# Attention before a routed expert layer: rounds of two score chunks, transposes a stage ahead, masks and shifts moved to other engines, one transfer for v

## The chip, the cores and the metric

One core of one Trainium2 chip. The metric is the device time of one execution in microseconds (us), the median of several; a profile of one execution goes with each kernel. Ratios between kernels are the mean time of one kernel's runs over that of the other's runs of the same rounds, so a ratio is not quite the ratio of the medians quoted beside it. Executions over 1.5% slower than the fastest of the same kernel are left out of the means.

Engines in the profile: PE is TensorE's matmuls, PEld its weight loads, DVE VectorE, ACT ScalarE, POOL GpSimd, SP SyncE; a q after a name means the engine's sequencer, which issues DMAs. In these traces an engine works through its own instructions in a fixed order: the two traced executions of the kernel before, almost 8 us apart in span, have the same order on every engine.

## The reference, cut to what matters

```python
B, H, S, D = 4, 8, 768, 64            # batch, heads, sequence, head width
scores = q @ k.T / sqrt(D)
# heads 0, 2, 6 ("retrieval"): causal mask
# heads 1, 3, 4, 5, 7 ("streaming"): causal, and only the last 64 keys or the first 4 ("sinks")
a = softmax(where(mask, scores, -1e9));  attn = a @ v
x = attn as [3072 tokens, 512]
out[tokens of expert e] = relu(x @ w1[e]) @ w2[e]     # 8 experts, 512 -> 1024 -> 512, one per token
```

## The kernel before

Heads go in pairs. For each pair q and k are transposed by TensorE and copied to SBUF, the on-chip memory for tiles (q by ACT, k by DVE; the copies are called qT and kT). Scores come out transposed (keys on the partitions), ACT takes the exponential, DVE multiplies by a mask, TensorE multiplies by v, which carries a column of ones for the sum of the row (this product is called AV below). The routing decides the slot of every token; POOL scatters the normalized rows there, the experts load them back slot by slot. "Pairs" are (0,2), (6,7), (1,3), (4,5), in that order, one stage each:

```python
def load_v(b):                                   # twelve transfers, issued by POOL
    for par in range(2):
        for t in range(NSO):
            nc.gpsimd.dma_start(out=ves[b][:, t, 4 * par : 4 * par + 4, 0:D], in_=v[b, par::2, ...])

def s_retr_pair(b, pi, c):                       # one chunk of scores of a causal pair
    ...                                          # 64-row matmuls of both heads into sc
    nc.scalar.activation(out=et[:, :, 448 * c : 448 * c + 448], in_=sc[:, :, 0:448], func=AF.Exp, scale=scale)
    for J in range(NSO):                         # the diagonal blocks' mask
        if 448 * c <= OFF[J] < 448 * c + 448:
            d = et[:, :, OFF[J] : OFF[J] + P]
            nc.vector.tensor_tensor(out=d, in0=d, in1=m_diag..., op=ALU.mult)

def vshift(b):                                   # v moved by 64 keys, for the streaming heads
    nc.vector.tensor_copy(out=vshs[b][0:64, ...], in_=ves[b][0:64, ...])
    nc.vector.tensor_copy(out=vshs[b][64:128, ...], in_=ves[b][64:128, ...])       # two of these

for b in range(B):
    ...
    for si, chunks in enumerate(stages):
        tq = t_units(b, si + 1) if si < 3 else (t_units(b + 1, 0) if b + 1 < B else [])
        per = -(-len(tq) // len(chunks)) if tq else 0
        for ci, (bud, f) in enumerate(chunks):
            f()                                  # scores, exponential, mask of one chunk
            for _ in range(per): ...             # transposes of the NEXT stage's pair
            run_a(bud)                           # some AV matmuls of earlier stages
        ...
        if si == 0: vshift(b)
...
load_w(wA, 2)                                    # POOL: weights of expert 2
load_x(0); load_x(1)                             # SP: rows of the first two experts
x_transpose(0)
load_w(wB, 3)
```

The softmax here doesn't subtract the row's maximum and nothing guards it: scores larger than these inputs give would overflow.

## Time and profile before

| | before |
|---|---|
| median of 4 runs | 269.31 us (268.14 to 271.21) |
| the profiled execution | 276.72 us, span 275.1 us |

From the profile's page of the kernel before: the span; busy time and share of each engine; TensorE's busy tenths in 40 equal slices; and the clock that TensorE was granted, in tenths of full speed.

```profile
span 275.1 us, 4932 instructions
...
PE 196.7 (72%) x1979; PEld 109.9 (40%) x1979; DVE 120.9 (44%) x340; ACT 92.5 (34%) x109; POOL 120.8 (44%) x191
...
PE   0279178783578478757600399999999999999940
...
PEclk9999999655696558855955569999999999999995
```

A slice is 6.9 us. The left half (to about 138 us) is attention, the two empty slices are the passage to the experts, and the rest is the experts at 90% and more. In attention no engine is full, and the clock is at 5 or 6 tenths most of the time. (The first digits of the clock row say nothing: this trace has no clock record before 46.6 us, and the transposes there took 0.31 us each, as in later stretches at half clock, against 0.22 at full clock.)

The waits of TensorE in attention, from the list of who waited for whom (total us, times, longest):

```profile
PE scs_2_0_453 L301 <- DVE kT_2_439 L218: 6.2, 1, 6.2
...
PE scs_2_0_946 L301 <- DVE kT_2_932 L218: 5.3, 1, 5.3
...
PE scs_2_0_1490 L301 <- DVE kT_2_1461 L218: 3.1, 1, 3.1
...
PE scs_2_0_1951 L301 <- DVE kT_2_1926 L218: 2.4, 1, 2.4
```

All four are the scores of the third stage, one per batch, waiting for DVE's copy of the transposed k. The timeline around the first (start, length, engine, line, what; idle time and its cause in brackets):

```profile
26.42 0.53 PE L205 MATMUL tpk_2_404<-ct,k_132 128*64 128x128 f16 x6
...
31.25 0.17 DVE L557 CAST r_loh<-r_lo 128x24 f16<-128x24 f32 x1
31.33 0.89 DVE L289 TENSOR_TENSOR eT_0_354<-eT_0_354,ct 128x128 f16<-128x128 f16 x6
32.14 0.55 DVE L340 TENSOR_TENSOR eS_0_416<-eS_0_416,m_str 128x768 f16<-128x768 f16 x1
32.61 0.95 DVE L218 COPY kT_2_439<-tpk_2_404 128x768 f16<-128x768 f16 x1
...
33.62 0.54 PE L301 MATMUL scs_2_0_453<-qT_2_388,kT_2_439 64*64 64x128 f16 x12 [6.22 <-DVE kT_2_439 L218]
```

The transposes were done at 27, the copy came at 32.6: it stood in DVE's queue behind a part of the routing (small operations until 31.4, the cast is the last of them) and then two sorts of masks. TensorE reached the scores and found no kT. In batch 1 the queue was held up otherwise, by a mask that waited for ACT's exponential:

```profile
64.76 0.56 DVE L340 TENSOR_TENSOR eS_1_909<-eS_1_909,m_str 128x768 f16<-128x768 f16 x1 [3.81 <-ACT eS_1_909 L337]
65.24 0.95 DVE L218 COPY kT_2_932<-tpk_2_895 128x768 f16<-128x768 f16 x1
```

### The profile page before, as it was taken

Reading aid. Unit: us, or ns where it says so; the run is one execution under the profiler, and the core shown is the slowest. Engines: PE = TensorE matmul, PEld = TensorE weight load, DVE = VectorE, ACT = ScalarE, POOL = GpSimd, SP = SyncE. Lnnn points to the kernel's source line nnn. Section 1 sums busy time; section 2 is a strip of 40 time slices with the busy share of each in tenths; the row PEclk is TensorE's granted clock in tenths of the full one; section 3 lists DMA queues with packets and bytes.
Section 4 is the critical chain, followed back from the end, with each engine's and each line's share of the span. In section 5 each row is a group of like instructions: output and inputs, shape, how many; then the busy total and the mean of one; then the engine's idle time right before and its main releaser. Section 6 shows DMA issues by size and latency. Waiting matters only on the chain. (4 is left out here: it accounts for less than half of the span.)

```text
span 275.1 us, 4932 instructions
## 1 busy us (share of the span) xinstructions
PE 196.7 (72%) x1979; PEld 109.9 (40%) x1979; DVE 120.9 (44%) x340; ACT 92.5 (34%) x109; POOL 120.8 (44%) x191
## 2 busy tenths in 40 slices
PE   0279178783578478757600399999999999999940
PEld 0235045352344255444500245544554545454410
DVE  0835953874799654976720103141413141413120
ACT  1186067333585158625000032404150505051400
POOL 8579398584725840242464001535344440504140
PEclk9999999655696558855955569999999999999995
DMA  7999999957999549510119999899999998202030
GB/s 134 236 172 137 182 60 170 155 98 141 193 203 138 97 85 187 95 60 19 50 70 168 239 230 224 206 213 270 213 276 229 272 229 215 112 4 92 17 112 1
DMA packets 55731, 41.27 MB, mean 150 GB/s; under 512 B 27901, under 2 KB 49301, under 8 KB 55703
## 3 DMA queue, kind: packets, MB, share of 16 engines
q0 software_dynamic: 50096, 35.67, 78.9%
q1 hardware_dynamic: 5606, 5.24, 6.9%
q8 instruction: 16, 0.26, 0.4%
q14 instruction: 13, 0.10, 0.1%
HBM read 56.64 MB, written 11.53 MB: 248 GB/s over the span
## 5 line engine op out<-in xcount | busy, mean ns | idle before, releaser
L400 POOL DMA_INDIRECT x_slots<-xb_1111,dest_i x6 | 6.7, 1122 | 23.1 <-DVE xb_1111 L451 20.9
L177 POOL DMA_DIRECT2D ve_1097<-in_v_dram x12 | 9.0, 772 | 10.0 <-DMA w_0_943<-in_moe_w_dram 3.7
L715 PE MATMUL tpx_0_2304<-ct,xe_2297 128*128 128x128 f16 x8 | 1.0, 311 | 16.8 <-DMA xe_2297<-x_slots 16.8
L177 POOL DMA_DIRECT2D ve_159<-in_v_dram x12 | 9.3, 804 | 4.8 <-DMA k_156<-in_k_dram 3.1
L177 POOL DMA_DIRECT2D ve_141<-in_v_dram x12 | 9.0, 762 | 4.9 <-DMA q_131<-in_q_dram 2.6
L749 POOL DMA_INDIRECT out_dram<-ob_2404,idx_i x1 | 1.0, 1049 | 22.8 <-DVE ob_2404 L748 22.8
L742 ACT ACTIVATE hT_2329<-h_0_0_2330 128x896 f16<-128x896 f32 x1 | 0.9, 917 | 30.0 <-PE h_0_0_2330 L735 30.0
L177 POOL DMA_DIRECT2D ve_600<-in_v_dram x12 | 8.9, 772 | 4.4 <-DMA k_597<-in_k_dram 3.1
L400 POOL DMA_INDIRECT x_slots<-xb_1633,dest_i x6 | 5.8, 972 | 6.4 <-DVE rcps_1_2183 L443 3.4
L715 PEld LDWEIGHTS <-xe_2297 128*128 128x128 f16 (+1 forms) x16 | 1.4, 138 | 17.1 <-DMA xe_2297<-x_slots 16.9
L400 POOL DMA_INDIRECT x_slots<-xb_614,dest_i x6 | 6.5, 1083 | 3.0 <-DVE xb_614 L451 1.8
L400 POOL DMA_INDIRECT x_slots<-xb_245,dest_i x6 | 6.1, 1024 | 1.5 <-issue 1.1
L719 DVE COPY xT_2303<-tpx_0_2304 128x1024 f16<-128x1024 f16 x1 | 0.7, 691 | 13.4 <-PE tpx_0_2304 L715 13.4
L488 PE MATMUL dom_ps<-ct,r_dlow 24*128 24x24 f16 x1 | 0.2, 197 | 8.3 <-DVE r_dlow L484 8.3
L735 PEld LDWEIGHTS <-w_0_941 128*128 128x128 f16 x32 | 3.8, 119 | 5.4 <-issue 3.8
L301 PE MATMUL scs_2_0_453<-qT_2_388,kT_2_439 64*64 64x128 f16 (+2 forms) x12 | 0.5, 311 | 6.2 <-DVE kT_2_439 L218 6.2
L719 DVE COPY xT_2370<-tpx_0_2371 128x1024 f16<-128x1024 f16 x1 | 0.7, 692 | 9.3 <-PE tpx_0_2371 L715 9.3
L749 POOL DMA_INDIRECT out_dram<-ob_3152,idx_i x1 | 1.0, 971 | 7.8 <-DVE ob_3152 L748 7.8
L749 POOL DMA_INDIRECT out_dram<-ob_3021,idx_i x1 | 1.0, 971 | 7.7 <-DVE ob_3021 L748 7.7
L735 PEld LDWEIGHTS <-w_1_1485 128*128 128x128 f16 x32 | 3.1, 98 | 3.0
L735 PEld LDWEIGHTS <-w_5_2578 128*128 128x128 f16 x32 | 3.1, 98 | 3.0
L735 PEld LDWEIGHTS <-w_7_2831 128*128 128x128 f16 x32 | 3.1, 98 | 3.0
(875 smaller groups left out, 650.8 us busy)
## 6 DMA issues: line engine op xcount, KB each, us to landing
x_slots<-zt SPq DMA_DIRECT2D x8, 128.0 KB, 8.0
w_0_941<-in_moe_w_dram POOLq DMA_DIRECT2D x1, 1024.0 KB
w_0_943<-in_moe_w_dram POOLq DMA_DIRECT2D x1, 1024.0 KB
w_1_1485<-in_moe_w_dram POOLq DMA_DIRECT2D x1, 1024.0 KB
w_1_1487<-in_moe_w_dram POOLq DMA_DIRECT2D x1, 1024.0 KB
w_2_2271<-in_moe_w_dram POOLq DMA_DIRECT2D x1, 1024.0 KB
w_2_2273<-in_moe_w_dram POOLq DMA_DIRECT2D x1, 1024.0 KB
w_3_2325<-in_moe_w_dram POOLq DMA_DIRECT2D x1, 1024.0 KB
```

What stands on the lines that cost most here:

```text
L177: nc.gpsimd.dma_start(out=ves[b][:, t, 4 * par : 4 * par + 4, 0:D], in_=v[b, par::2, t * P : (t + 1) * P, :].rearrange("h p d -> p h d"),)
L301: yield lambda g=g, a0=a0, a1=a1, hp=hp: nc.tensor.matmul(out=dst[hp : hp + 64, a0 - c0 : a1 - c0], lhsT=kT[b, pi][rows, 64 * g : 64 * g + ...
L400: ins = nc.gpsimd.indirect_dma_start(out=xs_dram, out_offset=bass.IndirectOffsetOnAxis(ap=dest_i[:, t : t + 1], axis=0), in_=xbs[b][:, it, :],
L488: nc.tensor.transpose(out=dps[:], in_=dlow[:], identity=ident[0:NT, 0:NT])
L715: nc.tensor.transpose(out=ps[:, j, c, 0:n], in_=xe[e][0:n, g, c * P : (c + 1) * P], identity=ident[0:n, 0:n])
L719: nc.vector.tensor_copy(out=xT[e][:, :, 0:256].rearrange("p c (j n) -> p c j n", j=2), in_=ps[:].rearrange("p j c n -> p c j n"),)
L735: nc.tensor.matmul(out=sc[:, j, 0:CAP], lhsT=w1t[:, c, ft * P : (ft + 1) * P], rhs=xT[e][:, c, :], start=(c == 0), stop=(c == 3),)
L742: nc.scalar.activation(out=hT[e][:, 2 * fp : 2 * fp + 2, :], in_=sc[:, :, 0:CAP], func=AF.Relu)
L749: ins = nc.gpsimd.indirect_dma_start(out=out, out_offset=bass.IndirectOffsetOnAxis(ap=idx_i[:, col : col + 1], axis=0), in_=ob[:], in_offs ...
```

## The change: intent and diff

The scores go in rounds: two chunks' score matmuls, then the masks of both, then both exponentials, then other work of TensorE ("fills"), so that matmuls of one tile shape stand side by side. The pairs' order is now (1,3), (4,5), (6,7), (0,2), and a pair's transposes are made a stage or more ahead, most of them in the last rounds of the batch before. The causal mask becomes a matmul that adds -30000 (identity times a mask block) to the scores in PSUM, the memory that TensorE writes its results to; the v shift goes from DVE to POOL, one scaling per streaming block from DVE to ACT. v of a batch comes by one transfer. Warm-up matmuls of zeros stand at the start and before the experts. The routing's arithmetic gets shorter. The diff, cut to its core (cuts are `...`):

```diff
-PAIRS = [(0, 2), (6, 7), (1, 3), (4, 5)]
+PAIRS = [(1, 3), (4, 5), (6, 7), (0, 2)]
...
-    c16[:, 128:256] = pp[:, None] <= pp[None, :]
+    c16[:, 128:256] = np.where(pp[:, None] <= pp[None, :], 0.0, NEG)
...
     def load_v(b):
-        for par in range(2):
-            for t in range(NSO):
-                nc.gpsimd.dma_start(... one sixth of four heads ...)
+        nc.gpsimd.dma_start(
+            out=ves[b][:, :, :, 0:D].rearrange("p h t d -> p (h t) d"),
+            in_=v[b].rearrange("h (t p) d -> p (h t) d", p=P),
+        )
...
+        def mask(n):
+            a0 = diag[n] - p0
+            nc.tensor.matmul(
+                out=dst[:, a0 : a0 + P], lhsT=ident, rhs=m_diag, start=False, stop=(n == len(diag) - 1)
+            )
...
-            for J in range(NSO):
-                if 448 * c <= OFF[J] < 448 * c + 448:
-                    d = et[:, :, OFF[J] : OFF[J] + P]
-                    nc.vector.tensor_tensor(... op=ALU.mult)
...
+    def run_round(chunks, fills):
+        for prods, _, _, _ in chunks:
+            prods()
+        for _, masks, _, _ in chunks:
+            if masks is not None:
+                masks()
+        for _, _, post, _ in chunks:
+            post()
+        for f in fills:
+            f()
+        for _, _, _, mult in chunks:
+            if mult is not None:
+                mult()
...
-                nc.vector.tensor_scalar(out=xbs[b][:, it, 4 * D : 5 * D], ...)
-                scatter_x(b, it)
+                nc.scalar.activation(out=xbs[b][:, it, 4 * D : 5 * D], ..., func=AF.Copy, scale=rcp[:, 0:1])
...
     def vshift(b):
-        nc.vector.tensor_copy(...)                       # three
+            nc.gpsimd.tensor_copy(...)                   # four
...
+    warm(10, "start")
...
+        vshift(b)
+        run_round([s_str_pair(b, 0, 0), s_str_pair(b, 0, 1)], r0 + (t02 if b == 0 else []))
+        run_round([s_str_pair(b, 1, 0), s_str_pair(b, 1, 1)], r1 + t_units(b, 3))
...
+        run_round([s_str_one(b, 2), s_sinks(b)], r2)
+        if b:
+            for t in range(NSO):
+                scatter_x(b - 1, t)
+        run_round([s_retr_pair(b, 3, 0), s_retr_pair(b, 3, 1)], [a_str_unit(b, 0)])
...
+        run_round([s_retr_pair(b, 3, 2), s_retr_pair(b, 3, 3)], [a_str_unit(b, 2)])
+        run_round([s_retr_pair(b, 3, 4), s_retr_pair(b, 3, 5)], [a_str_unit(b, 4)] + nt[0])
+        run_round([s_retr_one(b, 2, 0), s_retr_one(b, 2, 1)], a_retr_units(b, 0) + nt[1])
+        run_round([s_retr_one(b, 2, 2)], nt[2])
+        if b == 1:
+            routing_e()
+            routing_f()
+        carry = [a_retr_units(b, 2), a_retr_units(b, 6), []]     # AV of this batch in the next one's rounds
...
     load_x(0)
     load_x(1)
+    warm(16, "moe")
     x_transpose(0)
```

## The prediction

> **What bounds the kernel now.** The stretch table by engine splits the profiled 275.1 us in three. Attention runs to about 138 us (later batches 30 to 33 us each). To 155 TensorE is idle: last normalizations, scatters, loads of x. Then the experts keep it 100% busy to about 262; only their start can move. In attention no engine is full: in 43-138 us TensorE is busy 67.0 of 95 us, DVE 66.3, ACT 45.8. It is a chain of handovers. The list of waits shows TensorE waiting for kT copies 6.2, 5.3, 3.1, 2.4 us and four times about 1.9: the copy stands in DVE's queue behind masks that wait for ACT. TensorE is also slow: the clock row shows 0.6 to 0.75, and six transposes take 0.53 us cold, 0.36 warm. The Trainium skill, "TensorE: Matmul & The Clock Gate", Part 1, says that gaps in activity halve the clock; the trace agrees (half clock after the stages with such gaps).
>
> **What the change does.**
> 1. Transposes a stage ahead take the kT waits off the chain: about 8 us per batch.
> 2. Fewer changes of tile shape (177 before the experts; I count about 27 per batch after). The skill's "TensorEngine Tiling (Array Packing)", Key Properties, says that a change of mode drains the array. In the trace six transposes followed by scores occupy 0.46 us, of which 0.32 is streaming: 0.14 us a change, some 8 us in all, half of it hidden.
> 3. Diagonal masks leave DVE (2.7 us per batch) for 18 matmuls of 128 columns (about 1 us warm); the v shift (2.2 us) goes to POOL (perhaps 4 to 6 us there), six 0.28 us scalings to ACT. DVE falls from 20 to about 13.5 us per batch, ACT rises to 16.5.
> 4. One v transfer: POOL's 12 x 0.77 us become about 2 us; the same 6144 packets of 128 B, so DMA time (12.4 us x 16 engines per batch) stays. But no part of v is usable until all of it has landed.
> 5. Warm-up matmuls: the first expert ran cold from 157.4 to 162.7, worth at most 2.6 us.
>
> **Estimate.** A round costs two exponentials (1.83 us) plus about 0.75 us from exp end through the next scores and masks, partly filled by copies: 2.0 to 3.2 us, eight rounds 20.5 us. I take 21.5 for batches 1 to 3. Batch 0 gains little: its v lands near 25 us (q and k until 17.5), the shift ends near 30, the first streaming AV waits for it, so the batch ends near 42 (before: 43). Attention ends near 42 + 64.5 + 1.5 = 108. The tail grows: all six scatters of batch 3 now follow the last normalization (5 x 1.27 us more than the 12.5 us before), so experts start near 127 instead of 155; 2 us more for the warm clock. Saving about 30 us on 269.
>
> Predicted: 238 us, 8 in 10 between 224 and 253. Faster by over 2%: 0.94; within 2%: 0.04; slower: 0.02.
>
> **Signs.** Right: kT waits under 1 us; clock row mostly 0.9 or 1.0 in attention; batches 1 to 3 of 20 to 24 us; DVE about 25 us less; expert part about 107 us; batch 0 stalled at its first streaming AV on the shift or v.
>
> **What would make it wrong.** The clock stays cold (25 us per batch or more); the POOL shift is slow, blocks DVE, or stands behind DMA issues, so that streaming AV waits in every batch; rounds serialize worse; weights come late, as attention ends earlier. Faster: v lands earlier, or rounds approach ACT's 17 us.

## The result, and the profile after

| | before | after |
|---|---|---|
| median | 269.31 us | 246.02 us (244.47 to 246.17, 4 runs) |
| ratio | | 0.9116 (95%: 0.9051 to 0.9181) |
| the profiled execution | 276.72 us | 245.93 us, span 244.1 us |

The page after, the lines that answer to those above:

```profile
span 244.1 us, 5013 instructions
...
PE 187.0 (77%) x2077; PEld 108.3 (44%) x2077; DVE 98.0 (40%) x232; ACT 96.6 (40%) x133; POOL 109.6 (45%) x165
...
PE   6374269879748986880039999999999999999930
...
PEclk9657555799995799998557999999999999999985
```

A slice is 6.1 us now. Attention is shorter, the experts as long as before. DVE lost 23 us of work, ACT gained 4.

Where did the time go? The first trace of before was of an unusually long execution, so the comparison is with a second profile of the same kernel (run e1 below, span 267.4 us). The view of busy time by stretches, for that trace cut at the batches' ends, the end of attention, the first matmul of the experts (147.6) and the last of the eighth expert (16 left-over matmuls follow):

```profile
0.00:42.90 42.90, 19.32 (x258) 11.84 (x260) 23.48 (x83) 17.37 (x21) 30.59 (x45) 0.75 1.25 148
42.90:72.00 29.10, 23.11 (x320) 13.89 (x320) 21.34 (x55) 15.69 (x19) 22.74 (x33) 0.56 1.08 142
72.00:101.00 29.00, 20.55 (x345) 13.40 (x343) 22.80 (x75) 15.54 (x19) 13.88 (x22) 0.69 1.12 151
101.00:133.50 32.50, 25.07 (x426) 16.65 (x424) 23.94 (x76) 14.67 (x18) 10.96 (x20) 0.69 0.50 100
133.50:147.60 14.10, 0.00 (x0) 0.00 (x0) 0.00 (x0) 0.00 (x0) 6.15 (x10) 0.50 0.82 166
147.60:255.30 107.70, 106.97 (x626) 54.03 (x628) 27.94 (x51) 29.35 (x32) 34.48 (x59) 0.97 0.85 189
...
```

The columns are the stretch, its length, then busy us (and instructions) of PE, PEld, DVE, ACT, POOL, then granted clock, DMA share, GB/s. The same six stretches of after:

```profile
0.00:46.90 46.90, 29.26 (x420) 19.12 (x421) 24.13 (x67) 20.13 (x29) 27.35 (x34) 0.64 1.57 183
46.90:66.00 19.10, 15.15 (x370) 11.37 (x367) 16.27 (x39) 16.28 (x27) 13.32 (x18) 1.00 0.53 91
66.00:88.00 22.00, 17.58 (x354) 12.26 (x346) 15.70 (x47) 16.12 (x25) 11.49 (x18) 0.77 1.49 215
88.00:106.30 18.30, 14.64 (x315) 10.20 (x303) 12.73 (x30) 14.74 (x23) 10.75 (x17) 1.00 0.71 148
106.30:125.30 19.00, 2.57 (x12) 0.98 (x11) 0.00 (x0) 0.00 (x0) 9.69 (x16) 0.69 0.64 140
125.30:232.20 106.90, 106.09 (x626) 53.73 (x628) 27.87 (x51) 29.34 (x32) 34.67 (x59) 0.97 0.86 190
...
```

Batch 0 became 4 us longer. Batches 1 to 3 went from 29.1, 29.0 and 32.5 us to 19.1, 22.0 and 18.3, together 31 us less. The passage grew from 14.1 to 19.0, and the experts are as long as before (107.7, 106.9). ACT works 14.7 to 16.3 us in a batch, so batches of 18 to 19 us are near to what ACT alone would need.

What TensorE still waits for:

```profile
PE tpx_0_2291 L767 <- DMA xe_2267<-x_slots: 16.4, 1, 16.4
...
PE avs_0_441 L478 <- POOL vsh_123 L521: 4.7, 1, 4.7
...
PE scr_0_1488 L248 <- DVE kT_3_1433 L220: 3.2, 1, 3.2
...
```

The first is the wait for the experts' rows; the second batch 0's streaming AV, waiting for POOL's shift; the third the largest wait for a kT that is left, in batch 2, where the routing's last part (`routing_e` and `routing_f`) stands on DVE in front of the copy. The passage in the timeline:

```profile
105.26 3.61 PE L527 MATMUL warm_moe<-zt 128*128 128x512 f16 x16
...
114.43 0.84 POOL L127 DMA_DIRECT2D w_2_2241<-in_moe_w_dram  x1
...
116.10 0.38 SPq L747 DMA_DIRECT2D xe_2267<-x_slots  x1
116.16 0.80 POOL L127 DMA_DIRECT2D w_3_2312<-in_moe_w_dram  x1
...
125.30 0.93 PE L767 MATMUL tpx_0_2291<-ct,xe_2267 128*128 128x128 f16 x7 [16.43 <-DMA xe_2267<-x_slots]
```

The warm-up ends at 108.9, the first matmul of the experts comes at 125.3. The rows x are asked for at 116.1, in the midst of four weight transfers of 1 MB each, and take 9.2 us.

### The profile page after: what moved, and what is told of

Same layout as the page of the kernel before. It is cut to its first block, busy times and chain, and to the rows that moved or that the text cites. A ratio compares the mean times of both kernels' runs of the same rounds, so it can differ in the third digit from the quotient of the medians.

```text
span 244.1 us, 5013 instructions
## 1 busy us (share of the span) xinstructions
PE 187.0 (77%) x2077; PEld 108.3 (44%) x2077; DVE 98.0 (40%) x232; ACT 96.6 (40%) x133; POOL 109.6 (45%) x165
## 5 line engine op out<-in xcount | busy, mean ns | idle before, releaser
L801 POOL DMA_INDIRECT out_dram<-ob_2391,idx_i x1 | 1.1, 1053 | 21.3 <-DVE ob_2391 L800 21.3
L771 DVE COPY xT_2290<-tpx_0_2291 128x1024 f16<-128x1024 f16 x1 | 0.7, 690 | 20.2 <-PE tpx_0_2291 L767 20.2
L258 PEld LDWEIGHTS <-ct 128*128 128x128 f16 x72 | 4.9, 111 | 4.8 <-issue 4.8
L787 PEld LDWEIGHTS <-w_0_990 128*128 128x128 f16 x32 | 3.4, 109 | 4.7 <-issue 2.5
L527 PEld LDWEIGHTS <-zt 128*128 128x128 f16 x26 | 2.7, 111 | 5.1 <-issue 2.0
L527 PE MATMUL warm_start<-zt 128*128 128x512 f16 x10 | 3.8, 556 | 1.3 <-DVE zt L669 1.3
L186 DVE COPY vs_sink<-vpat 128x1320 f16<-128x1320 f16 x1 | 2.2, 2232 | 6.3 <-DMA vpat<-vpat_c 6.3
L478 PEld LDWEIGHTS <-eS_0_1_321 128*64 128x64 f16 x24 | 1.9, 150 | 6.5 <-issue 6.5
L191 POOL DMA_DIRECT2D vs_sink<-in_v_dram x5 | 2.9, 577 | 4.0 <-DMA k_136<-in_k_dram 2.1
L180 POOL DMA_DIRECT2D ve_158<-in_v_dram x1 | 2.2, 2216 | 5.1 <-DMA ve_145<-in_v_dram 5.1
L801 POOL DMA_INDIRECT out_dram<-ob_3139,idx_i x1 | 1.0, 980 | 7.8 <-DVE ob_3139 L800 7.8
L787 PEld LDWEIGHTS <-w_7_2818 128*128 128x128 f16 x32 | 3.1, 98 | 3.0
L787 PEld LDWEIGHTS <-w_5_2565 128*128 128x128 f16 x32 | 3.1, 98 | 3.0
L787 PEld LDWEIGHTS <-w_1_1533 128*128 128x128 f16 x32 | 3.1, 98 | 3.0
L787 PEld LDWEIGHTS <-w_3_2312 128*128 128x128 f16 x32 | 3.1, 98 | 3.0
```

The source lines that it names most:

```text
L180: nc.gpsimd.dma_start(out=ves[b][:, :, :, 0:D].rearrange("p h t d -> p (h t) d"), in_=v[b].rearrange("h (t p) d -> p (h t) d", p=P),)
L186: nc.vector.tensor_copy(out=vs_sink[:], in_=vpat[:].unsqueeze(1).to_broadcast([P, B, 5, VW]))
L191: nc.gpsimd.dma_start(out=vs_sink[r0 : r0 + 4, :, SIDX[h], 0:D], in_=v[:, h, 0:4, :].rearrange("b s d -> s b d"),)
L258: nc.tensor.matmul(out=dst[:, a0 : a0 + P], lhsT=ident, rhs=m_diag, start=False, stop=(n == len(diag) - 1))
L478: nc.tensor.matmul(out=pss[it][hp : hp + 64, s, 0 : D + 1], lhsT=et[:, 64 * a : 64 * a + 64], rhs=rhs[:, 0 : D + 1], start=(it == 0), stop ...
L527: nc.tensor.matmul(out=ps[:, i % 2, :], lhsT=zt[:, 0:P], rhs=zt[:], start=True, stop=True)
```

## The experiments

Theories. (T) The early transposes carry the gain: kT no longer arrives late. Rivals: (S) the grouping of tile shapes, each change of which the prediction put at 0.14 us; (C) the clock, as TensorE ran at half speed most of the time; (M) the work taken off DVE; (V) the transfer of v and the place of its shift. No run takes apart the shorter routing, the order of the pairs, the later scatters or the streaming AV in pairs of blocks. Twelve kernels ran; the results of all were correct against the reference.

| run | what | median us | ratio to before (95%) |
|---|---|---|---|
| after | the change | 246.02 | 0.9116 (0.9051 to 0.9181) |
| e1 | before, again | 267.76 | 0.9959 (0.986 to 1.0057) |
| e2 | before, transposes two stages ahead | 256.58 | 0.9564 (0.9494 to 0.9633) |
| e3 | before, filler matmuls in the waits | 273.11 | 1.0153 (1.0078 to 1.0227) |
| e4 | after, transposes one round ahead | 256.72 | 0.9571 (0.9488 to 0.9655) |
| e5 | after, shapes mixed | 249.78 | 0.9308 (0.924 to 0.9375) |
| e6 | after, diagonal masks on DVE | 255.02 | 0.9494 (0.9425 to 0.9563) |
| e7 | after, v shift on DVE | 245.35 | 0.9141 (0.905 to 0.9232) |
| e8 | after, v in 12 transfers | 266.20 | 0.9902 (0.9824 to 0.998) |
| e9 | e6 with the masks later in DVE's queue | 249.54 | 0.9335 (0.9276 to 0.9395) |
| e10 | e8 with the shift on DVE | 248.71 | 0.9285 (0.9213 to 0.9357) |
| e11 | after, no warm-ups | 246.57 | 0.9202 (0.9137 to 0.9267) |
| e12 | a better version | 236.70 | 0.8859 (0.8798 to 0.892) |

Runs e1 to e4, e5 to e8 and e9 to e12 shared their runs of before (medians 269.07, 268.77, 267.06), and after was timed beside others still (269.31). A difference of 2 us between groups is therefore not a result, and the distances from after given below are good to about 2 us.

### e1: the kernel before once more

No edit.

> The kernel before, unchanged, once more with a profile. The profiled run of before took 276.7 us, while its timed runs take 268.1 to 271.2; the profiled run of after took 245.9, as its timed ones. If that trace of before was an unusually long execution (theory A), this profiled run takes 268 to 271 us and its span about 268, and the lost time shows in one stretch. If profiling itself makes this kernel longer (rival B), it takes 275 to 278 again.

Measured: 267.76 us, span 267.4. Theory A holds: no timed run of before went over 271.21, so the first traced execution, at 276.72, stands alone. The kernel's first expert matmul came at 147.6 us, not 154.9. Most of the difference arose in batch 1 (32.5 us from its first exponential to that of batch 2, against 29.2) and between the last exponential and the last normalization (11.9 us against 8.3). In just these two places the first trace has waits that the profile puts down to a sender it does not know ("remote"): ACT 3.6 us before the exponential that the mask shown above waits for, DVE 2.1 us before the last reciprocal. None of the other 13 traces has such a wait. What these waits were stays open.

### e2: one part alone, the transposes, in the kernel before

```diff
-            tq = t_units(b, si + 1) if si < 3 else (t_units(b + 1, 0) if b + 1 < B else [])
+            n2 = 4 * b + si + 2
+            tq = t_units(n2 // 4, n2 % 4) if n2 < 4 * B else []
...
-    for c, f in t_units(0, 0):
+    for c, f in t_units(0, 0) + t_units(0, 1):
```

> The kernel before with one part of the change alone: transposes two stages ahead instead of one, so that kT is ready when its scores come. Theory: the waits for kT (19 us by the first listing, 27 with the weight loads' share) are the largest part of the gain; expected 250 to 258 us, ratio 0.93 to 0.96. Rival (the gain comes from tile shapes, masks and clock): 264 to 269 us, the waits turn up at the next thing in DVE's queue.

Measured: 256.58 us, ratio 0.9564, and the waits for kT are gone from TensorE's list (in e1 they add up to 23.3 us, 18.1 of them in the third and fourth stages, and to 3 to 4 us in each of batches 1 to 3). A change of two lines brings more than half of the gain, without a word about tile shapes (TensorE changes shape 177 times before the experts in this trace, as in the first trace of before), masks or the clock (granted 0.804 over the span, against 0.789 in e1; recorded at full clock for 30.7 us before the experts in both).

### e3: the clock alone

```diff
+                if ci == 0 and si in (2, 3):
+                    filler(12 if si == 2 else 5, f"{b}_{si}")     # matmuls of zeros
                 f()
```

> The kernel before with matmuls of zeros (12 and 5 per batch) in the places where TensorE waits for kT, to keep its clock up and for nothing else. Theory that the slow clock of attention is what the change removed: attention's granted clock rises to over 0.9 and the time falls by 8 us or more. Rival (the clock follows from the waits, and the time is set by handovers between DVE, ACT and TensorE): the clock rises, the time stays within 3 us of before, or grows.

From its page:

```profile
span 272.1 us, 5068 instructions
...
PEclk9999997658989597979955579999999999999995
```

The clock rose, though not to over 0.9: the trace's clock records have TensorE at full clock for 71.7 us before the experts, against 30.7 in e1. The time grew by 1.5% (interval 0.8 to 2.3%). So theory C falls as the main cause: twice the time at full clock bought nothing here. e2 and e4 (below) say the same: they take the same time, 256.6 and 256.7 us, with 30.7 and 68.3 us at full clock before the experts. (The fillers themselves can stand in the way, so a gain of a few us from the clock is not excluded.)

### e4: the transposes late again, in the kernel after

```diff
-    run_round([s_str_pair(b, 0, 0), s_str_pair(b, 0, 1)], r0 + (t02 if b == 0 else []))
-    run_round([s_str_pair(b, 1, 0), s_str_pair(b, 1, 1)], r1 + t_units(b, 3))
+    run_round([s_str_pair(b, 0, 0), s_str_pair(b, 0, 1)], r0 + (t01 if b == 0 else t_units(b, 1)))
+    run_round([s_str_pair(b, 1, 0), s_str_pair(b, 1, 1)], r1 + t_units(b, 2))
...                                   # pair 3 in round 3, pair 0 of the next batch in the last round
```

> The kernel after with its transposes only one round ahead (each pair in the fills of the round before the one that needs it), all else as after. If the early transposes carry the gain: 255 to 262 us against 246, with waits for kT back at two to three us per batch and stage. Rival (rounds of one tile shape carry it): 246 to 250 us.

Measured: 256.72 us, 10.7 more than after, with 16.7 us of TensorE waiting for kT in attention. The largest entry for a kT in its list of waits:

```profile
PE scs L326 <- DVE kT L220: 8.9, 6, 3.6
```

The same step is worth 12.5 us added to before (269.07 to 256.58) and 10.7 us taken from after: T holds from both sides, for about half of the 23 us. It is the only part that was both added to before and taken from after. The other half is not shared out: the parts below were only taken from after, and what they cost there (3.8, 9 and 20 us) adds up to more than the gain.

### e5: the grouping of shapes

```diff
+        for prods, masks, post, _ in chunks:
+            prods()
+            if masks is not None:
+                masks()
+            post()
+            for f in fl[:per]:
+                f()
+            fl = fl[per:]
```

> The kernel after with each chunk followed at once by its masks, its exponential and its half of the fills, so that matmuls of one tile shape no longer stand side by side; transposes as early as in after. If the grouping is worth what I counted (74 fewer changes of shape, 0.1 to 0.14 us each, half hidden): 249 to 253 us. If the grouping is worth nothing once kT is ready: 244 to 247 us, or faster, as the first exponential of a round starts earlier.

Measured: 249.78 us, in the range of the first theory; in its trace the experts start only 1.5 us later than in after (126.8 against 125.3). TensorE changes shape 148 times before the experts against 101 in after. The 3.8 us over 47 changes are 0.08 us each, which is neither an upper nor a lower bound, as the start of the exponentials and the place of the fills moved too. S is small.

### e6 and e9: the diagonal masks, and their place in the queue

e6 multiplies by the mask on DVE straight after the exponential, as before did, and leaves the mask matmuls out. e9 does the same work, but issues the multiplies at the end of the round (the slot called mult in `run_round`).

```diff
 # e6, in post()                            # e9
             nc.scalar.activation(... Exp)
+            for J in range(NSO):           # the same loop in mult()
+                if 448 * c <= OFF[J] < 448 * c + 448:
+                    d = eR[b, pi][:, :, OFF[J] : OFF[J] + P]
+                    nc.vector.tensor_tensor(out=d, in0=d, in1=m_diag..., op=ALU.mult)
```

> The kernel after with the diagonal masks as multiplies on DVE again (2.7 us per batch) instead of 18 matmuls per batch. If DVE's queue is what delays: 249 to 252 us. If DVE has slack by now (it is busy 16 of 20 us a batch): 244 to 248 us, and the exponentials start some 0.4 us earlier per round, which may even gain a few us.

Measured: 255.02 us, slower than both expected ranges and 9 us more than after, for about 2.7 us of DVE work per batch. DVE is not full (77.1 us busy in the first 134). The timeline of one round of e6 shows why (names without numbers in this trace):

```profile
55.48 1.72 ACT L285 ACTIVATE eT<-scr 128x896 f16<-128x896 f32 x2
...
57.23 0.29 DVE L291 TENSOR_TENSOR eT<-eT,ct 128x256 f16<-128x256 f16 x1 [1.95 <-ACT eT L285]
...
57.44 0.19 DVE L498 RECIPROCAL rcps<-avs 128x5 f32<-128x5 f32 x1
...
58.18 0.31 ACT L506 ACTIVATE xb<-avs,rcps 128x64 f16<-128x64 f32 x1 [0.98 <-DVE rcps L498]
...
58.74 0.31 ACT L506 ACTIVATE xb<-avs,rcps 128x64 f16<-128x64 f32 x1 [0.24 <-DVE xb L500]
...
58.95 0.91 ACT L285 ACTIVATE eT<-scr 128x896 f16<-128x896 f32 x1
```

DVE sits 1.95 us idle before the mask, which waits for the second exponential; the reciprocals of AV results that were there long ago stand behind it; ACT's scalings wait for the reciprocals, and the next round's exponentials stand behind the scalings. The round is a loop through two queues. If that reading is right, moving the masks behind the reciprocals should free the loop:

> As the run with masks on DVE (255.0 us), but each round's masks stand in DVE's queue after the round's reciprocals and scalings, not before them. In that run a round was a loop: second exponential, its mask, then the reciprocals behind it on DVE, then the scalings on ACT, then the next exponentials behind those. If the place in the queue was what cost 9 us (theory): 244 to 248 us, though DVE does the same work. If DVE's 2.7 us per batch of work cost it (rival): 252 to 256 us again.

Measured: 249.54 us. That misses the range by 1.5 us but takes back 5.5 of the 9 us with the same DVE work. The two were timed in different groups, and by their ratios it is about 4 of 10 us; in the traces attention's last exponential ends at 113.0 us in e6, 106.4 in e9 and 104.8 in after. So the place in the queue is the larger part of M in the traces, not the amount of work. What remains (3.5 us) is not settled: e9 is level with after up to the end of batch 2 (87.3 and 87.7 us) and loses 2.0 us in the last batch, where its clock fell for 10 us.

### e7, e8, e10: v and its shift

e7 has the shift on DVE, issued just before its first use. e8 has v in 12 transfers again. e10 has both.

```diff
 # e7
-            nc.gpsimd.tensor_copy(out=vshs[b]...
+            nc.vector.tensor_copy(out=vshs[b]...
 # e8
-        nc.gpsimd.dma_start(out=ves[b][:, :, :, 0:D]..., in_=v[b]...)
+        for par in range(2):
+            for t in range(NSO):
+                nc.gpsimd.dma_start(out=ves[b][:, par::2, t, 0:D], in_=v[b, par::2, t * P : (t + 1) * P, :]...)
```

> The kernel after with the shift of v on DVE (2.2 us per batch, issued just before its use) instead of POOL (3.8 us). Batch 0 waits 4.7 us for the POOL shift after v has landed: with DVE the shift should take some 2 us there. Expected, if that wait is on the chain: 243 to 245 us for batch 0 alone, but 2 us of DVE in every later batch may cost it back: 244 to 250 us. If POOL's shift were slowing DVE[...], this version would be clearly faster, below 242 us.

Measured: 245.35 us, no difference that these runs could show (ratios 0.9141 and 0.9116). In its trace batch 0's exponentials ended at 42.7 us (after: 46.4), batch 1 took 18.5 us (17.0), batch 3 18.4 (16.6): about half of the gain at the start is given back, and the experts start at 123.3 us (125.3). So for this kernel POOL's shift is no gain over DVE's by itself.

> The kernel after with v of a batch in 12 transfers again. The same packets, so the DMA time stays; POOL issues for 9 us instead of 2 and waits for earlier transfers, which puts the shift of v later. Expected 247 to 251 us, with the wait for the shift longer in batch 0 and later. If the one transfer is itself what delays v (all of it must land before the first use): 242 to 245 us.

Measured: 266.20 us. Almost the whole gain is gone, four times the most that I expected. POOL's timeline:

```profile
31.87 0.74 POOL L182 DMA_DIRECT2D ve<-in_v_dram  x1 [1.32 <-DMA q<-in_q_dram]
...
35.70 3.73 POOL L182 DMA_DIRECT2D ve<-in_v_dram  x5 [3.09 <-DMA k<-in_k_dram]
...
39.47 1.50 POOL L523 COPY vsh<-ve 64x1584 f16<-64x1584 f16 x1
...
42.90 0.21 PE L480 MATMUL avs<-vsh,eS 128*64 128x65 f16 x1 [16.89 <-POOL vsh L523]
```

The copy for batch 0's shift stands in POOL's queue behind the issues of batch 1's transfers. POOL issued q, k and six pieces of v, then waited for q to land before the next, and for k before the one after: in this program at most eight transfers are under way from that queue (k landed at 35.4, and the next piece of v went at 35.7). With one transfer for v this limit costs less but is still met: in after POOL waits 5.1 us, until batch 0's v lands at 23.9, before it issues batch 1's, and the shift stands behind that issue and starts at 26.2. Batch 0's exponentials end at 59.8 instead of 46.4 us.

> v in 12 transfers together with the shift on DVE. In the run with 12 transfers the POOL shift stood behind transfers that POOL could not yet issue (16.9 us in batch 0); with the shift on DVE nothing of attention stands behind them. If the one transfer matters only because the shift is on POOL (theory): 244 to 248 us, as with the shift on DVE alone (245.4). If 12 transfers delay the data of v itself (rival): 252 us or more.

Measured: 248.71 us, ratio 0.9285, just above the theory's range. So the 12 transfers cost 20 us with the shift on POOL and 3.4 us with the shift on DVE (e10 against e7). The two edits belong together: putting work on POOL only pays if POOL's queue does not stand still. The 3.4 us are in the tail: in e10 one scatter of the last batch waits 3.2 us on POOL for an earlier scatter.

### e11: the warm-up matmuls

```diff
-    warm(10, "start")
-    warm(16, "moe")
```

> The kernel after without its two groups of warm-up matmuls. In its trace the clock had fallen again before attention's scores (at 7.8 us) and before the experts (at 113.6, their first transposes at 125.3), so I expect 245 to 247 us, no difference. If the start group matters for the first transposes: 1 to 2 us slower.

Measured: 246.57 us, as expected no difference that these runs could show (ratios 0.9202 and 0.9116, their intervals overlap). The clock records of after: full from 4.4 to 7.8 us, then half; in the end full from 82.9 to 113.6, then half until 130.6. The start group's effect is over before the first scores at 14.6, and the second group's is over 11.7 us before the experts begin.

### e12: a version that beats both

```diff
+        if b == 0: vshift(b)           # on DVE, just before its use; later batches on POOL as in after
...
-        if 0 < b < 3:
-            load_w(wA, b - 1)
+        if b:
+            load_w(wA, b - 1)          # expert 2 too, in the last batch
...
-        if b == 1:
-            routing_e()
-            routing_f()
...
-    load_w(wA, 2)
+    routing_e()                        # behind attention
+    routing_f()
...
-    warm(16, "moe")
+    warm(64, "moe")
     x_transpose(0)
+    nc.gpsimd.tensor_copy(out=junk[:, 0:8], in_=xe[1][0:1, 0, 0:8])     # POOL waits for x
     load_w(wB, 3)
```

> The kernel after with what its trace still shows on the chain taken away: shift of batch 0 on DVE (about 3.5 us), weights of expert 2 loaded in attention's last batch and those of expert 3 only once x of the first two experts has landed, so that x, issued at 116.1 and landed at 125.3, does not share the DMA engines with them (about 5 us), the routing's last part moved behind attention (3.2 us wait for kT in batch 2), 64 instead of 16 warm-up matmuls so that they last until x lands (about 2.5 us). Sum about 14: expected 232 us, 229 to 237. If x takes as long to land without the weights: about 237 to 239.

Measured: 236.70 us, ratio 0.8859 to before, at the slow end of the range: of the 14 us expected the traces show 10. The passage in its timeline:

```profile
102.23 13.98 PE L528 MATMUL warm_moe<-zt 128*128 128x512 f16 x64
...
114.13 0.38 SPq L749 DMA_DIRECT2D xe<-x_slots  x1
...
117.20 1.06 PE L769 MATMUL tpx<-ct,xe 128*128 128x128 f16 x16 [1.00 <-DMA xe<-x_slots]
```

x lands 3.1 us after it is asked for instead of 9.2, with the weights out of its way. The experts then run at full clock from the first matmul and take 104.9 us instead of 106.8. From the two traces (244.1 and 234.1 us): batch 0 ends 2.9 us earlier, the passage from the last normalization to the experts is 4.4 us shorter (14.7 against 19.1), the experts 1.9, batch 2 with the gap before it 3.5; batch 3 is 2.7 us longer, with TensorE at half clock from 90.1 to 100.3.

## Why the prediction was right, and where it was off

The direction, the range and the main mechanism (kT in front of the scores) were right; the size of that mechanism was not, and the centre was 8 us too low (238 against 246.0). Point by point:

- **kT waits.** "About 8 us per batch" was more than twice too much for this part alone: e2 and e4 show that the early transposes by themselves carry 11 to 12 of the 23 us, 3 us per batch, and e1 has waits of 3 to 4 us in each of batches 1 to 3. These batches did lose 7 to 14 us each (29 to 32 us became 18 to 22), but by all parts together. Three waits over 1 us were left (3.2, 1.4 and 1.1), against the sign "under 1 us".
- **Tile shapes.** Counted: about 27 changes per batch, so 108; measured 101. Expected 8 us in all, half hidden; e5 measured 3.8 us, for 47 of the 76 changes that went.
- **Masks, shift.** I counted DVE's work (20 to 13.5 us per batch; over attention it fell from 91.6 to 68.8 us, my sign said 25) and left out its order. The traces of e6 and e9 show that the order is worth more than the work.
- **One v transfer.** I gave it no gain in time. That is right only next to the old place of the shift: with the shift on POOL it is what keeps the change from costing 20 us (e8, e10).
- **Batch 0.** Predicted: v near 25 us, shift near 30, end near 42. Measured: v by 23.9, shift from 26.2 and in use at 29.6, end 46.4. The wait was seen ahead; the 4 us more come after it (ACT waits another 2.9 us for reciprocals on DVE in this batch, where the routing's arithmetic also stands).
- **Batches 1 to 3.** Predicted 64.5 us, measured 58.4 from exponential's end to exponential's end.
- **Passage.** Predicted: experts start near 127. Measured: 125.3. That this is so close is partly luck: batch 0 took 4.4 us more and batches 1 to 3 took 6.1 us less than predicted.
- **The step that failed** is "experts start near 127 instead of 155". The 127 was good to 2 us. The 155 came from a trace of an execution that was 7.4 us longer than the ones being predicted, and I took the difference of 28 us off the time of the others, 269. In an ordinary execution (e1) the experts start at 147.6, so the right difference was 147.6 - 127 = 20.6 us, which gives 269 - 20.6 = 248. Both numbers stood side by side from the beginning: the profiled run 276.7, the timed ones 268 to 271.
- **The warm clock.** "2 us more" did not come: the warm-up ended 16 us before it was needed (e11). Long enough, it brings 1.9 us (e12).
- **The clock as a danger.** In after TensorE is at full clock for 64.9 us of 125, against 30.7 of 147.6. What raised it is not shown; it was not the removed kT waits alone, as e2 has none and stays at 30.7, and e4 has them back and keeps 68.3. e3 speaks against the clock as the main cause. The Trainium skill, "TensorE: Matmul & The Clock Gate", Part 1, has it that activity raises the clock and gaps lower it; the traces agree, in steps of 3.4 us. In the 14 traces each of the 83 falls follows a step in which TensorE was busy at most 78% of the time, each of the 69 rises one with at least 81%. Not every busy step brings a rise: in e2 the clock stays at half from 48.6 to 65.7 us with TensorE busy 88 to 100% of each step. My sign "mostly 0.9 or 1.0" held in batches 1 and 3 (1.00), not in batch 0 (0.64) and batch 2 (0.77).

## What to carry to other kernels

When several engines hand tiles to each other and none is full, look at what stands in front of the late instruction in its engine's queue; issuing a producer a stage earlier, or a consumer's multiply behind work that is already ready, added no work and was worth more here than shorter work, a faster clock or fewer changes of shape. A queue that issues transfers is a bad place for work that others wait for, unless few transfers keep it moving. And before taking differences between traces, check that the traced execution took as long as the timed ones.

## What the Trainium skill lacked or had wrong

- "TensorE: Matmul & The Clock Gate", Part 1: it does say how soon a warm-up is lost, with one measured run in which the clock fell 5.2 us after the last matmul. The trace of after agrees: the clock fell at 113.6 us, 4.7 us after the last of 16 warm-up matmuls (108.9), and the work came at 125.3; 64 of them, ending 1 us before the work, kept the clock, and the experts took 1.9 us less (e12). What it lacks is a warning that a faster clock may be worth nothing: with fillers that brought 71.7 us at full clock instead of 30.7 the kernel took 1.5% longer (e3).
- "TensorEngine Tiling (Array Packing)", Key Properties: says that changing the mode drains the array, without a figure. Here a version with 47 more changes of shape took 3.8 us longer, 0.08 us for each on average (e5).
- "DMA: Bandwidth & Descriptors", Issuing engines are not separate DMA queues: the section has transfers from all queues share the 16 DMA engines. It gives no figure for what a late small transfer pays: the first 384 KB of x took 9.2 us between four weight transfers of 1 MB and 3.1 us without them (e12).
- "SBUF — State Buffer", SBUF: two separate sides, says that DVE and POOL block each other on a shared port. The trace of after agrees: a DVE multiply of 0.17 us took 0.97 us while POOL copied, and ended within 0.02 us of POOL's copy. The first and third lines are DVE's, the second POOL's:

```profile
63.47 0.17 DVE L224 TENSOR_TENSOR kbd<-kT_1_1193,ct 128x8 f16<-128x8 f16 x1
...
65.19 1.50 POOL L521 COPY vsh_123<-ve_476 64x1584 f16<-64x1584 f16 x1
...
65.74 0.97 DVE L224 TENSOR_TENSOR kbd<-kT_2_1236,ct 128x8 f16<-128x8 f16 x1
```

  What it lacks is a sense of size in a whole kernel: with the shift on DVE instead (e7) the time was the same, 245.35 us.
- No page that I read names a limit of transfers under way from one queue; here POOL stops at eight in flight until the oldest has landed (e8, and for 5.1 us in after), which may be the program's own doing. The run shows the waits, not their origin.
